# Transposes on TensorE at the start, chunks of last tokens between the parts of Wo, and a later half of the row statistics

## The chip, the core and the metric

The kernel runs on one core of one Trainium2 chip. The metric is the device time of one execution in microseconds (us); shown is the median of three runs. One further execution was recorded by the hardware profiler; all times of single instructions come from it. The names of the engines are those of the profile: PE is TensorE (matmuls), PEld its weight loads, DVE VectorE, ACT ScalarE, POOL GpSimd, SP SyncE (which issues DMAs).

## What is computed

A residual stream x of 2048 rows with 512 columns passes four layers: A, B, A, B, each on the layer-normalised x.

```python
def A(x, mem, Wq, Wk, Wv, Wo):            # H = 32 heads of 128, 8 memory rows, segments of 32 rows
    for s in range(64):
        h = concat([mem, x[32*s : 32*s+32]])              # 40 rows
        q, k, v = h @ Wq, h @ Wk, h @ Wv                  # 512 -> 32 x 128 each
        p = softmax(mask(q @ k.T * scale))                # a memory row sees all 40 rows
        o = (p @ v) @ Wo                                  # 4096 -> 512
        mem, out[s] = o[:8], o[8:]                        # the next segment needs mem
def B(x):                                  # gated MLP that mixes rows
    z = gelu(x @ w_in); z1, z2 = halves(z)
    return (z1 * (w_sp @ layernorm(z2) + b_sp)) @ w_out
x = x + A(ln(x)); x = x + B(ln(x)); x = x + A(ln(x)); x = x + B(ln(x))
```

Layer A is a recurrence over 64 segments: segment s + 1 cannot start its projections before segment s has put out its memory rows. All heads' weights stay in SBUF: Wq, Wk and Wv with 4 MB each, Wo with 4 MB.

## The kernel before

**Layer A** is `a_block` (from L653), called once per A layer; `first` is true for the first. Rows come in 16 tiles of 128 rows (`tb`), four segments to a tile (`j4` = 0 to 3). `_Rows.apply` (L193) normalises a tile with mean and reciprocal deviation and has it turned by a DMA transpose (L201) into `hT`, whose columns are the rows of x; 32 columns ahead of them hold the memory rows. Segment s uses 32 columns of `hT`: 8 of memory and 24 of its rows. The last 8 rows of each segment ("last tokens") don't fit in 32 columns; their projections are made for a whole tile at once: `ln_turn` copies the tile's 32 last tokens out of `hT` into `hB` (L620), and `b_units` (L736) multiplies them with Wq, Wk and Wv in six chunks of 16 matmuls (`psb` at L697), two each. The chunks of the next tile are spread over the segments of the present one as fillers: `fill()` takes the next unit of a generator, `more`, at three places of a segment (L1035, L1041, L1070; in the first segment at L1013 and L1024 instead). Chunks alternate between two accumulators in PSUM, `accA` and `accB`; `accB` also serves `psm`, `psV` and `px` of the segment. What must be read out of a chunk waits in the list `copies` and is run at set places, on ScalarE (L758 or L751). For the first tile it is then turned on VectorE (`turns`, L761) or regrouped; for others by a DMA transpose on SP (L763), and V goes through DRAM (`store_v`, `spread_v`).

**A segment** (L889 to L1079) runs on PE in this order: `psQ`, `psm`, `psK` (queries and keys), `psK`/`psV` (values), `psS` (scores), `psO` (sums and outputs), `psT`, then Wo: `px` (L777, heads 0 to 17, in pairs) and `psO` columns 384 to 511 (L784, heads 18 to 31). VectorE and ScalarE fold the parts of px together (`cross` L1053 and L873, `t1` L875), add the rest (`memT` L880) and turn it into the next segment's memory columns (`hT` L881), on which the next `psQ` waits. `Rt` (L1055, L1058) are the reciprocal sums, with which `tok_out` and `last_out` scale the outputs (L997, L1000).

The order of PE, VectorE and ScalarE is that of the program text; POOL and SP keep theirs by the same text but are not part of the hand-written schedule.

**The start.** SP loads the first two row tiles and the memory rows. POOL issues the weight loads in this order: halves 0 of Wq and Wk, halves 1 of Wq and Wk, both halves of Wv, four parts of Wo (heads 0 to 14) and three parts of `Wo_high` (heads 15 to 22, 23 to 30, 31). The two row tiles are normalised and turned by DMA (L201), the memory rows too (L522). `_consts` makes masks and the identity for transposes (L60 to L65) after that. Then the block runs ahead: chunks 0 and 2 of tile 0, chunks 0 and 2 of tile 1, chunks 1 and 3 of tile 0 (L1084 to L1090; the numbers are j of `b_units`: 0 and 1 Wq, 2 and 3 Wk, 4 and 5 Wv). Segment 0 fills with chunks 4 and 5 of tile 0, segments 1 and 2 with the other four of tile 1 (`units1`, L1118).

**Row statistics.** In the first block, segments with j4 = 1 compute mean and variance of the tile after the next: `x_stats` with k = 0 (first half of the columns, L141, in `spare1`), k = 1 (second half, in `spare2`, L1158) and k = 2 (both put together, L143, in `spare3`, L1167). `spare2` stands ahead of `fold` (L1062), `spare3` behind `build_hA` (L1064) and `store_o`. In segments with j4 = 1 of some tiles `spare2` also adds half of a row tile of y (`y_half`, L229).

```python
            run(turns)
            spare2()
            t1 = wk.tile([P, P], F32, name="t1", bufs=1)
            fold(px, cross, t1, beside)
            if s + 1 < NSEG:
                build_hA(s + 1, pw, t1)
            if s > 0:
                store_o(s, pw, t1)
            spare3()
            tok_out(0)
```

## Time and profile before

| | us |
|---|---|
| median of 3 runs (1649.05, 1649.40, 1654.26) | 1649.4 |
| the profiled execution | 1649.51 |
| its span, first to last instruction | 1647.8 |
| first matmul | 17.62 |
| psQ of segment 0, of segment 1 | 32.11, 53.68 |
| psQ of segment 2, of segment 3, of segment 4 | 65.16, 75.32, 85.24 |

In a line of the timeline stand the start (us from the span's start), the time that the instructions took, engine, line of the kernel, operation, output <- inputs, shape, count, and in brackets the idle time of the engine before it with what ended it. Neighbouring instructions of one kind are merged into a line. In a line of the windows stand the stretch, its length, the busy time and number of instructions of each engine (PE, PEld, DVE, ACT, POOL), the granted TensorE clock as a share, the busy share of the 16 DMA engines and GB/s. In the groups of the page stand busy time, mean time of one instruction in ns, and idle time of the engine just before them. Lines of DMA queues give packets, MB and the share of 16 engines' time in the stretch; q0 are the DMAs that POOL issues, q1 those that SP issues.

### The profile page before, as it was taken

Reading aid. Unit: us, or ns where it says so; the run is one execution under the profiler, and the core shown is the slowest. Engines: PE = TensorE matmul, PEld = TensorE weight load, DVE = VectorE, ACT = ScalarE, POOL = GpSimd, SP = SyncE. Lnnn points to the kernel's source line nnn. Section 1 sums busy time; section 2 is a strip of 40 time slices with the busy share of each in tenths; the row PEclk is TensorE's granted clock in tenths of the full one; section 3 lists DMA queues with packets and bytes.
Section 4 is the critical chain, followed back from the end, with each engine's and each line's share of the span. In section 5 each row is a group of like instructions: output and inputs, shape, how many; then the busy total and the mean of one; then the engine's idle time right before and its main releaser. Section 6 shows DMA issues by size and latency. Waiting matters only on the chain.

```text
span 1647.8 us, 87178 instructions
## 1 busy us (share of the span) xinstructions
PE 1590.4 (97%) x39122; PEld 953.7 (58%) x39122; DVE 1183.4 (72%) x2924; ACT 1072.7 (65%) x2278; POOL 289.2 (18%) x604
## 2 busy tenths in 40 slices
PE   4799999999999999999999999999999999999999
PEld 1455555555665666566655565556556666554565
DVE  3677777778887787884467777777788778877722
ACT  2577777777777777661047777777777777776400
POOL 5111111111211122320011111111122112214000
PEclk9999999999999999999999999999999999999999
DMA  9312221212222234276952121112233123335796
GB/s 353 101 42 42 43 42 44 44 42 74 78 55 45 73 84 87 87 190 139 211 168 46 46 45 46 49 46 44 60 88 85 46 58 94 97 63 153 150 198 162
DMA packets 264734, 149.06 MB, mean 90 GB/s; under 512 B 198680, under 2 KB 240784, under 8 KB 264360
## 3 DMA queue, kind: packets, MB, share of 16 engines
q1 hardware_dynamic: 251128, 99.66, 27.6%
q0 software_dynamic: 13232, 43.82, 8.2%
q8 instruction: 307, 5.03, 1.3%
q14 instruction: 67, 0.55, 0.1%
HBM read 59.68 MB, written 37.19 MB: 59 GB/s over the span
## 4 chain that ended last, share of the span: by engine, by line
PE 55%; DVE 2%; issue 0%; ACT 0%; DVEq 0%
PE pg L388 9%; PE psQ L697 7%; PE psK L697 7%; PE psb L697 5%; PE pz L287 5%; PE px L777 4%; PE psm L697 3%; PE psV L697 3%; PE psO L784 3%; PE py L431 2%; PE pwB L796 2%; PE psO L958 1%; PE psO L975 1%; PE psT L967 1%; PE psS L932 1%; PE pw L1211 0%
## 5 line engine op out<-in xcount | busy, mean ns | idle before, releaser
L697 PEld LDWEIGHTS <-hT 128*32 128x32 bf16 x12288 | 339.8, 97 | 299.9 <-DVE hT L881 27.8
L909 DVE STREAM_TRANSPOSE QQ<-rows 128x512 bf16<-128x512 bf16 x256 | 177.6, 694 | 60.0 <-ACT rows L906 59.0
L909 DVE STREAM_TRANSPOSE KA<-rows 128x512 bf16<-128x512 bf16 x256 | 176.0, 688 | 11.6 <-ACT rows L906 6.1
L997 DVE TENSOR_TENSOR uT<-psO,Rt 128x384 bf16<-128x384 f32 x256 | 141.0, 551 | 36.6 <-ACT Rt L1058 35.6
L906 ACT CAST rows<-psQ 128x512 bf16<-128x512 f32 x256 | 142.8, 595 | 28.3 <-PE psQ L697 25.2
L388 PE MATMUL pg<-z,wspT 128*128 128x344 bf16 x1024 | 154.3, 309 | 0.0
L1058 ACT ACTIVATE Rt<-Rt 128x512 f32<-128x512 f32 x256 | 147.2, 622 | 4.0
L697 PE MATMUL psQ<-Wq_sb,hT 128*32 128x512 bf16 x2048 | 136.0, 383 | 10.7 <-DVE hT L881 6.7
L941 ACT ACTIVATE S<-psS 128x224 bf16<-128x224 f32 x256 | 91.5, 358 | 80.6 <-PE psS L936 80.5
L994 DVE TENSOR_TENSOR uT<-psO,Rm 128x128 bf16<-128x128 f32 x256 | 74.7, 292 | 96.6 <-ACT Rm L993 95.9
L867 POOL COPY KX<-old 128x128 bf16<-128x128 bf16 x128 | 70.2, 548 | 392.3 <-PE psS L936 272.7
L777 PEld LDWEIGHTS <-uT 128*32 128x32 bf16 x4608 | 110.5, 96 | 47.5 <-DVE uT L994 31.7
L697 PE MATMUL psQ<-Wk_sb,hT 128*32 128x512 bf16 x2048 | 135.7, 382 | 0.0
L777 PE MATMUL px<-Wo,uT 128*32 128x256 bf16 x3840 | 134.7, 274 | 0.2 <-DMA Wo<-in_A_Wo_dram 0.2
L697 PE MATMUL psm<-Wq_sb,hT 128*32 128x512 bf16 x2048 | 134.4, 379 | 0.0
L697 PE MATMUL psK<-Wk_sb,hT 128*32 128x512 bf16 x2048 | 134.4, 379 | 0.0
L697 PE MATMUL psK<-Wv_sb,hT 128*32 128x512 bf16 x2048 | 134.3, 379 | 0.0
L697 PE MATMUL psV<-Wv_sb,hT 128*32 128x512 bf16 x2048 | 133.6, 378 | 0.0
L784 PE MATMUL psO<-Wo_high,uT 128*32 128x128 bf16 x7168 | 126.7, 220 | 7.0 <-issue 4.4
L1055 ACT ACTIVATE Rt<-psT 128x1024 f32<-128x1024 f32 x128 | 131.2, 1025 | 3.2
L867 POOL COPY KX<-front 128x128 bf16<-128x128 bf16 x126 | 67.5, 542 | 373.2 <-PE psS L936 238.0
L388 PEld LDWEIGHTS <-wspT 128*128 128x128 bf16 x1024 | 100.2, 98 | 53.2
(190 smaller groups left out, 2867.2 us busy)
## 6 DMA issues: line engine op xcount, KB each, us to landing
o_d<-o_sb SPq DMA_DIRECT2D x126, 64.0 KB
vb_d<-front SPq DMA_DIRECT2D x30, 256.0 KB
VX<-vb_d SPq DMA_DIRECT2D x120, 64.0 KB
ln_x<-xd SPq DMA_DIRECT2D x26, 256.0 KB
y_o<-o_d POOLq DMA_DIRECT2D x22, 256.0 KB, 3.3
xd<-y_o POOLq DMA_DIRECT2D x22, 256.0 KB, 2.9
Wq_sb<-in_A_Wq_dram POOLq DMA_DIRECT2D x8, 512.0 KB, 9.3
Wk_sb<-in_A_Wk_dram POOLq DMA_DIRECT2D x8, 512.0 KB, 11.0
```

The costliest lines, as they stand in the source:

```text
L287: nc.tensor.matmul(pz[:, c0:c1], lhsT=xnT[:, kt, :], rhs=w_in_sb[:, kt, c0:c1], start=(kt == 0), stop=(kt == KT - 1))
L388: nc.tensor.matmul(pg[t][:, k, 0:344], lhsT=wsp[t][:, st, :], rhs=z(st, 344 * k, 344 * k + 344), start=(st == 0), stop=(st == NT - 1))
L697: return [nc.tensor.matmul(ps[32 * cg:32 * cg + 32, :], lhsT=lhs(kt, cg), rhs=rhs(kt, cg), start=(kt == 0), stop=(kt == KT - 1), tile_posi ...
L777: nc.tensor.matmul(px[at:at + 32, 0:256], lhsT=lhs[:, h, :], rhs=wo_rhs(h, slice(k + 2, None, -2) if h % 2 else slice(k, None, 2)), start= ...
L784: nc.tensor.matmul(pw[32 * cg:32 * cg + 32, :], lhsT=lhs[:, h, :], rhs=wo_rhs(h, cg), start=False, stop=(h == H - 1), tile_position=(0, 32 ...
L867: eng.tensor_copy(KX[:, :, r].rearrange("p g (k i) -> p i g k", i=4), bs["KTB"][:, r].rearrange("p (i g) k -> p i g k", i=4)[:, :, :, 8 * ...
L906: return r, mms, nc.scalar.copy(r[:], ps)
L909: nc.vector.transpose(out=QQ[:, j % 2, :, 0:32] if j < 2 else KA[:, j % 2], in_=r[:])
L941: return nc.scalar.activation(out=S[:, r], in_=psS[:, r, 0:224], func=ACT.Exp, scale=scale)
L997: nc.vector.tensor_tensor(out=hview(uT_nxt[:], r, 0, 24), in0=oview(r, 8, 32), in1=rview(r, 0, 24), op=ALU.mult)
L1055: nc.scalar.activation(out=Rt[:], in_=psT[:], func=ACT.Ln)
L1058: nc.scalar.activation(out=rt, in_=rt, func=ACT.Exp, scale=-1.0)
```

## The change

Three things, all in layer A of the first block.

1. The identity for transposes is made directly in bf16 and before the first tiles are normalised. For the first two row tiles and the memory rows, `apply` gets a function `turn`: four TensorE transposes of 128 columns each into a PSUM tile, and one copy on ScalarE into `hT` (or `m0T`). The three DMA transposes are gone. In the text, `turn` of a tile stands between its normalisation and the statistics of the next.
2. `units1` (tile 1's last tokens) gets `alone=True`: all chunks use `accA`, each is one unit, its copy follows it. Two of its chunks still run in the prologue. Of the other four, two run in segment 0 ahead of px and two between heads 22 and 23 of Wo, that is between the first and the second part of `Wo_high`; each is followed by its copy on ScalarE, and for the first two by the DMA transposes on SP. Segments 1 and 2 get no fillers.
3. `x_stats` with k = 1 moves from `spare2` to `spare3`.

```diff
@@ _ln_consts
+    c["ident_bf"] = _identity(nc, cp)
...
+def _identity(nc, cp):
+    ident_bf = cp.tile([P, P], BF16, name="ident_bf")
+    nc.gpsimd.memset(ident_bf[:], 0.0)
+    nc.gpsimd.affine_select(out=ident_bf[:], in_=ident_bf[:], compare_op=ALU.not_equal, fill=1.0,
+                            base=0, pattern=[[-1, P]], channel_multiplier=1)
+    return ident_bf
@@ _Rows.apply
-    def apply(self, tb, MV, RS, first=False, x=None):
+    def apply(self, tb, MV, RS, first=False, x=None, turn=None):
...
-        nc.sync.dma_start_transpose(out=t[:, :, 32:32 + P], in_=xn[:].rearrange("t (kt s) -> t kt s", s=P))
+        if turn is None:
+            nc.sync.dma_start_transpose(out=t[:, :, 32:32 + P], in_=xn[:].rearrange("t (kt s) -> t kt s", s=P))
+        else:
+            turn(t[:, :, 32:32 + P], xn[:], P)
@@ the kernel's start
-        nc.sync.dma_start_transpose(out=rows.m0T[:], in_=m0[:].rearrange("t (kt s) -> t kt s", s=P))
...
-        for tt in range(2):
-            _stats(nc, rp, rows.xs[tt], MV[0][:, tt, :])
-            _rstd_act(nc, RS[0][:, tt:tt + 1], MV[0][:, tt, 1:2], c)
-            rows.apply(tt, MV[0], RS[0], first=True)
+        with tc.tile_pool(name="turn_ps", bufs=3, space=PSUM) as turn_ps:
+
+            def turn(out, x, n):
+                ps = turn_ps.tile([P, KT * n], BF16, name=f"turn{n}", tag="turn")
+                for kt in range(KT):
+                    nc.tensor.transpose(ps[:, n * kt:n * kt + n], x[:, P * kt:P * kt + P], c["ident_bf"][0:n, 0:n])
+                nc.scalar.copy(out, ps[:].rearrange("p (kt t) -> p kt t", kt=KT))
+
+            for tt in range(2):
+                _stats(nc, rp, rows.xs[tt], MV[0][:, tt, :])
+                _rstd_act(nc, RS[0][:, tt:tt + 1], MV[0][:, tt, 1:2], c)
+                rows.apply(tt, MV[0], RS[0], first=True, turn=turn)
+            turn(rows.m0T[:], m0[:], 2 * M)
@@ b_units
-        def b_units(tb, early=0):
+        def b_units(tb, early=0, alone=False):
...
-                ps = (accB if k % 2 and not (now and j == 5) else accA).tile([P, 512], F32, name="psb")[:]
-                for kts in (((0,), (1, 2), (3,)), ((0, 1, 2, 3),))[k % 2]:
+                ps = (accB if k % 2 and not alone and not (now and j == 5) else accA).tile([P, 512], F32, name="psb")[:]
+                for kts in (((0,), (1, 2), (3,)), ((0, 1, 2, 3),))[k % 2 or alone]:
...
-                        elif j == 4:
+                        elif j == (5 if alone else 4):
                             store_v(bs)
...
-                if now or k % 2:
+                if now or k % 2 or alone:
                     yield
@@ wo_rest
-        def wo_rest(pw, lhs):
+        def wo_rest(pw, lhs, lo=WO_PAIR, hi=H):
-            for h in range(WO_PAIR, H):
+            for h in range(lo, hi):
@@ segment
             run(copies)
+            if first and s == 0:
+                ahead_of_wo()
             px = accB.tile([P, 512], F32, name="px")
             wo_pairs(px, uT_cur)
             pw = psO[0][:, 0, 384:512]
-            wo_rest(pw, uT_cur)
+            if first and s == 0:
+                wo_rest(pw, uT_cur, hi=wo.low + 8)
+                ahead_of_wo()
+                wo_rest(pw, uT_cur, lo=wo.low + 8)
+            else:
+                wo_rest(pw, uT_cur)
@@ the prologue of the block
-            units, units1 = b_units(0, 6), b_units(1, 2)
-            for gen in (units, units1, units):
-                for _ in range(4):
+            units, units1 = b_units(0, 6), b_units(1, 2, alone=True)
+            for gen, n in ((units, 4), (units1, 2), (units, 4)):
+                for _ in range(n):
...
+        def ahead_of_wo():
+            for _ in range(2):
+                next(units1)
+                run(copies)
@@ the loop over segments
+            elif first and s == 1:
+                more = iter(())
             elif j4 == (first and tb == 0):
-                more = units1 if first and s == 1 else b_units(tb + 1)
+                more = b_units(tb + 1)
@@ spare2, spare3
-                if first and j4 == 1 and tb + 2 < NB:
-                    x_stats(tb + 2, 1)
...
                 if first and j4 == 1 and tb + 2 < NB:
+                    x_stats(tb + 2, 1)
                     x_stats(tb + 2, 2)
```

More of the change, by code (lines that the diff above doesn't have):

```diff
@@ L59, in _consts @@
     tmp = tctx.enter_context(tc.tile_pool(name="consts_tmp", bufs=1))
-    ident_f = tmp.tile([P, P], F32, name="ident_f")
-    nc.gpsimd.memset(ident_f[:], 0.0)
-    nc.gpsimd.affine_select(out=ident_f[:], in_=ident_f[:], compare_op=ALU.not_equal, fill=1.0,
-                            base=0, pattern=[[-1, P]], channel_multiplier=1)
-    ident_bf = cp.tile([P, P], BF16, name="ident_bf")
-    nc.vector.tensor_copy(ident_bf[:], ident_f[:])
     maskf = tmp.tile([P, 224], F32, name="maskf")
@@ L99, in _consts @@
     tctx.close()
-    c.update(ident_bf=ident_bf, maskN=maskN, ones=ones)
+    c.update(maskN=maskN, ones=ones)
     return c
```

## The prediction

> **What bounds the kernel now.** Read first the page: how full is TensorE, and what does the chain that ended last consist of?
>
> ```profile
> span 1647.8 us, 87178 instructions
> PE 1590.4 (97%) x39122; PEld 953.7 (58%) x39122; DVE 1183.4 (72%) x2924; ACT 1072.7 (65%) x2278; POOL 289.2 (18%) x604
> ```
>
> TensorE works 97% of the span. Moving work can pay only where TensorE idles or runs slowly. Its timeline over the first 100 us shows such a place, segment 0 and the start of segment 1:
>
> ```profile
> 38.87 0.40 PE L697 MATMUL psb<-Wv_sb,hB 128*32 128x512 bf16 x4 [0.83 <-DMA Wv_sb<-in_A_Wv_dram]
> 40.17 0.40 PE L697 MATMUL psb<-Wv_sb,hB 128*32 128x512 bf16 x4 [0.90 <-DMA Wv_sb<-in_A_Wv_dram]
> ...
> 44.12 0.23 PE L958 MATMUL psO<-E,ones 64*128 64x64 bf16 x4 [2.20 <-DVE E L944]
> ...
> 44.76 0.84 PE L777 MATMUL px<-Wo,uT 128*32 128x256 bf16 x24
> 45.78 0.40 PE L777 MATMUL px<-Wo,uT 128*32 128x256 bf16 x6 [0.18 <-DMA Wo<-in_A_Wo_dram]
> 48.78 0.40 PE L777 MATMUL px<-Wo_high,uT 128*32 128x256 bf16 x6 [2.61 <-DMA Wo_high<-in_A_Wo_dram]
> 48.91 0.55 PE L784 MATMUL psO<-Wo_high,uT 128*32 128x128 bf16 x20
> 51.80 1.15 PE L784 MATMUL psO<-Wo_high,uT 128*32 128x128 bf16 x36 [2.34 <-DMA Wo_high<-in_A_Wo_dram]
> 53.68 1.90 PE L697 MATMUL psQ<-Wq_sb,hT 128*32 128x512 bf16 x16 [0.74 <-DVE hT L881]
> ```
>
> Every step to 51.80 is paced by weights that land; the chain is the load stream and then the last heads of Wo. The stages say whether that stream is full (last two columns) and what the clock does (third last):
>
> ```profile
> 5.00:10.00 5.00, 0.00 (x0) 0.00 (x0) 2.81 (x11) 0.50 (x2) 4.49 (x15) 1.00 1.00 308
> 42.70:46.10 3.40, 1.80 (x48) 1.13 (x48) 1.86 (x6) 0.59 (x2) 0.44 (x2) 1.00 1.02 347
> 46.10:49.50 3.40, 0.75 (x28) 0.50 (x26) 0.28 (x1) 0.26 (x1) 0.00 (x0) 1.00 1.03 347
> 49.50:52.90 3.40, 1.10 (x36) 0.88 (x35) 0.29 (x1) 2.17 (x3) 0.00 (x0) 0.50 0.22 72
> 52.90:56.30 3.40, 2.66 (x32) 1.01 (x32) 1.96 (x7) 0.59 (x1) 0.00 (x0) 0.50 0.00 0
> ```
>
> The DMA engines are busy without a break (share 1.00 and more) to 49.5. After a stretch with 0.75 us of matmuls the granted clock falls to 0.50, and stays there into segment 1, whose first 16 matmuls take 1.68 us (53.68 to 55.36) where others take 0.86.
>
> Now the segments that the change touches, cut at the first psQ matmul of each: segments 1, 2, 3, and three with j4 = 1.
>
> ```profile
> 53.68:65.16 11.48, 11.48 (x292) 6.20 (x296) 8.23 (x21) 6.29 (x14) 1.40 (x3) 0.88 0.01 4
> 65.16:75.32 10.16, 10.16 (x296) 5.84 (x292) 7.18 (x19) 8.18 (x20) 1.50 (x3) 1.00 0.25 36
> 75.32:85.24 9.92, 8.64 (x266) 5.24 (x258) 7.55 (x19) 7.76 (x18) 1.51 (x3) 1.00 0.27 76
> 340.53:350.69 10.16, 10.16 (x299) 5.95 (x294) 8.08 (x22) 7.91 (x18) 1.49 (x3) 1.00 0.20 61
> 381.96:392.34 10.38, 10.33 (x297) 5.90 (x293) 8.65 (x24) 8.14 (x18) 3.14 (x6) 1.00 0.36 109
> 587.91:598.29 10.38, 10.33 (x296) 5.80 (x295) 9.08 (x26) 8.39 (x20) 3.13 (x6) 1.00 0.37 120
> ```
>
> The third row matters most: segment 3 has no unit of last tokens in it, 30 matmuls fewer, and is only 0.24 us shorter. A segment without such a unit waits 1.28 us (9.92 - 8.64) where one with a unit computes. **So taking units out of segments 1 and 2 saves almost nothing by itself.**
>
> **Part 1, turning by TensorE.** Three DMA transposes go (two row tiles, memory rows). Two things could follow: last tokens are ready earlier, and the load stream is relieved. First the price of the replacement, from the places where the kernel does the same:
>
> ```profile
> L407 PE MATMUL pT<-ident_bf,front x12: 219/219/229, 839.1 to 1641.9; 128*128 128x128 bf16 x12
> L408 ACT COPY front<-pT x2: 800/808/817, 840.1 to 1642.2; 128x768 bf16<-128x768 bf16 x2
> ...
> 17.27 0.30 ACT L620 COPY hB<-hT 128x128 bf16<-128x128 bf16 x1 [10.79 <-DMA hT<-ln_xn]
> ```
>
> Four transposes and a copy of 512 columns are about 0.6 + 0.6 us a tile, all while TensorE has nothing (its first matmul is at 17.62) and ScalarE has been idle 10.79 us. The second tile's statistics now queue behind the first's copy on ScalarE, which I follow to hB at 11.3 us instead of 17.27 and 24.20. Cost nothing; the cover is 6 us. Nor does earlier hB gain by itself, since the weights of its units land later than that. The gain is the stream:
>
> ```profile
> q0 software_dynamic: 1404, 5.10, 92.9%
> q1 hardware_dynamic: 1261, 0.39, 12.1%
> ...
> q0 software_dynamic: 1573, 5.73, 102.8%
> ```
>
> The first two rows are 10 to 24.2 us, the last 24 to 38. Queue q1 takes 12.1% of 14.2 us, 1.72 us, of which a load of 128 KB is 0.32 at 410 GB/s: 1.4 us for the transposes. The other way: 5.10 MB at the later 5.73/14.0 are 12.46 us instead of 14.2, less 0.32: 1.42. I take 1.4; the bounds are 0 (the stream was held elsewhere) and 1.75.
>
> In segment 0, Wv's last piece then lands at 38.8 instead of 40.17, the prologue (whose last chunks waited for no weights) is ready before that, and the px step is reached at 43.4 instead of 44.76. Against that, two transposes of rowsB are now issued on SP in segment 0, ahead of Wo's end. In segment 1 to 2 (66 to 69.5 us) they and an o_d store took this:
>
> ```profile
> q1 hardware_dynamic: 653, 0.19, 47.6%
> ```
>
> That is 1.67 us of all engines. They start about 46 and 48 us and drain at q1's 12% beside q0, so of the last 3 us of Wo they cost 0.3; bounds 0 and 1.67.
>
> **Part 2, four chunks between the parts of Wo.** A chunk is 16 matmuls, 0.86 us (32.99 to 33.85 in the timeline). All four use one accumulator, so the next waits for the copy: 0.59 us, and I add 0.2 us around it.
>
> ```profile
> 28.68 0.59 ACT L758 CAST rowsB<-psb 128x512 bf16<-128x512 f32 x1 [1.12 <-PE psb L697]
> 49.50 1.02 ACT L1055 ACTIVATE Rt<-psT 128x1024 f32<-128x1024 f32 x1
> 52.99 0.29 DVE L880 TENSOR_TENSOR memT<-psO,t 128x128 bf16<-128x128 f32 x1 [3.10 <-PE psO L784]
> ```
>
> First pair: 43.4 + 0.86 + 0.8 + 0.86 = 45.9; the 30 px matmuls to 46.7; the wait for Wo_high's first part ends at 48.78 - 1.4 = 47.4. Then 26 matmuls to 48.0 and the second pair to 50.5. The last part would land at 51.8 - 1.4 + 0.3 = 50.7. One thing speaks against it:
>
> ```profile
> q8 instruction: 307, 5.03, 1.3%
> ...
> q8 instruction: 1, 0.02, 6.8%
> ```
>
> 307 packets for 78244 TensorE instructions (matmuls and weight loads) are one per 255: these are TensorE's own instructions, and one (33 to 34 us, 6.8% of 16 engines) holds one DMA engine 1.09 us. Before, the third came at 50.4, after the loads. Now 24 instructions of turning (12 transposes, each with a weight load) and 64 of the first pair run ahead of px, so it comes 88 instructions, 44 matmuls, sooner: of the 56 matmuls between 44.76 and 49.4 only 12 stay ahead of it. It falls near 47 us, while the last part is on its way, and that engine's share lands 1.1 us later: 51.7. I take this.
>
> The 36 matmuls then run at full clock, since TensorE now works in the gaps: 0.7 us instead of 1.15. The copy of the fourth chunk and cross on ScalarE end at 51.6, before the matmuls (with the early landing they would end later and set the end, at 52.6 in place of 53.1, and Rt's 1.02 us behind them would then cost segment 1 about 0.5: the same sum). memT and its turn take 0.7: psQ at 53.1. Gain **0.55**; bounds -0.5 and 1.6.
>
> Segment 1 at full clock and without units is a segment 3: 9.92 instead of 11.48, **1.56**; bounds 0 and 1.56. Segment 2 becomes one as well: **0.24**; bounds 0 and 0.25.
>
> **Part 3, the second half of the row statistics.** It stands on VectorE ahead of cross in 14 segments (j4 = 1, first block). Segment 37:
>
> ```profile
> 431.98 0.42 DVE L141 BATCH_NORM_STATS2 bnst<-ln_x 128x6 f32<-128x256 bf16 x1
> 432.16 0.26 ACT L1053 COPY cross<-px 64x128 f32<-64x128 f32 x1 [0.76 <-PE px L777]
> ...
> 432.43 0.28 DVE L873 COPY cross<-px 64x128 f32<-64x128 f32 x1
> ...
> 432.72 0.39 PE L697 MATMUL psb<-Wq_sb,hB 128*32 128x512 bf16 x4
> ...
> 433.16 1.05 PE L697 MATMUL psb<-Wk_sb,hB 128*32 128x512 bf16 x16
> ```
>
> VectorE starts cross 0.27 us after ScalarE started its half, and the Wk chunk (same accumulator as px) starts 0.22 us late. Only the segments that also add a half of y have it: four, 381.96 the first and 587.91 the last, 0.22 over the usual 10.16. Elsewhere statistics end 0.1 us before px does and moving them gains nothing. 4 x 0.21 = **0.84**; bounds 0 and 1. Later, the 0.42 us stand ahead of tok_out, where VectorE then idles about a microsecond for the next segment's rows: nothing.
>
> **Sum.** The profiled execution took 1649.51 (span 1647.8), 0.1 over the median of 1649.4. 0.55 + 1.56 + 0.24 + 0.84 = 3.2, so 1646.3 for it and **1646.2** beside the median.
>
> **Rivals.**
> *The clock falls again.* Around the last landing TensorE works about 1.3 us in 3.4. The rows have full clock kept after 1.80 us in 3.4 and lost after 0.75; between them nothing is shown. If it falls, segment 1 keeps its 1.56: 1647.8. The Trainium skill ("TensorE: Matmul & The Clock Gate", Part 1: The HAM clock gate) has the gate close after an idle window of about 3.4 us; by that rule this rival would be out. But the rows 46.10 to 52.90 lose the clock after a window that was not idle, so it keeps a chance.
>
> *Slower: the chunks run at half clock.* If the prologue, thinner now, leaves TensorE at 0.50 through segment 0, each chunk takes 1.72. Px begins at 43.4 + 4.3 = 47.7, Wo_high's 26 matmuls end at 50.1, the second pair at 54.4, the last heads at 55.5, psQ at 56.2, 2.6 late; segments 1 and 2 give back 0.25 each, part 3 0.84: 1650.7. It decides as soon as half clock lasts past 43 us. Against it: from psQ on (32.11 before, earlier now) segment 0 has five chunks in a row that wait for no weights, 8 us at half clock, and 2.66 us in 3.4 were enough at 52.90 to 56.30.
>
> *More than the sum.* Had the transposes also slowed 5 to 10 us (308 GB/s against 410 later), another 1.25 comes with them. And TensorE waits for its own issue inside Wo's heads:
>
> ```profile
> L784 PE MATMUL psO<-Wo_high,uT 128*32 128x128 bf16 x7168 | 126.7, 220 | 7.0 <-issue 4.4
> ```
>
> Those 4.4 us hang on where instruction packets end in a segment, and 24 instructions shift that everywhere. If a third goes as well: 1646.2 - 1.25 - 1.4 = 1643.6. It can as well rise by as much.
>
> *Part 3 only moves the wait* (tok_out late, then the next rows): 1647.0. Against it stands VectorE's idle time there.
>
> **Chances.** Forecast 0.50; more than the sum 0.22; clock falls 0.13; part 3 moves the wait 0.07; half clock 0.08. The range takes the lower bounds (1.6 + 1.56 + 0.25 + 1 and the issue waits, 5.8: 1643.5, and some scatter) and reaches to the slower rival: 1643 to 1650.6. 0.3% (4.9 us, about what a measurement of this kernel can tell from no change; one of its three runs was 4.9 over the others) lies at 1644.5 and 1654.3. Faster by more: the third rival and the low end of the forecast, 0.28; slower by more: only the half clock with an unlucky run, 0.06; within: 0.66.
>
> **What would show it.** Right: no DMA wait of hB; TensorE's wait for Wv still there but ending about 38.8; chunks at 43 to 50 with two waits for Wo_high much shorter; PEclk 1.00 from 35 to 60; segments 1 and 2 at 9.9; segments 33, 37, 49, 53 at 10.2. Wrong: Wv's last wait still at 40.2 (the stream gained nothing), PEclk 0.50 anywhere in 43 to 60, psQ of segment 1 later than 53.7, or DVE late in segments 34, 38.

## The result, and the profile after

On one chip the changed kernel took 1645.05 us (median of 10 runs, 1641.75 to 1648.32) and the kernel before 1649.68 (10 runs, 1648.57 to 1654.56). The ratio is 0.9967, 95% interval 0.9955 to 0.9978: 5.4 us less by the ratio (3.6 to 7.4), 4.6 by the medians. The forecast was 3.2. The profiled execution took 1644.70, with a span of 1643.0.

| psQ of segment | 0 | 1 | 2 | 3 |
|---|---|---|---|---|
| before | 32.11 | 53.68 | 65.16 | 75.32 |
| after | 30.38 | 53.85 | 63.87 | 73.90 |

Segment 0 ends 0.2 us later than before, where 0.55 earlier was forecast; segments 1 and 2 give 1.45 and 0.13. The timeline of TensorE shows why. Lines of the kernel after stand some 13 higher than before (L697 is now L710, L777 L790, L784 L797, L881 L894); L536 is the new transpose:

```profile
6.53 0.59 PE L536 MATMUL turn<-ident_bf,ln_xn 128*128 128x128 bf16 x4 [6.53 <-POOL ident_bf L59]
...
30.38 1.90 PE L710 MATMUL psQ<-Wq_sb,hT 128*32 128x512 bf16 x16 [1.70 <-DVE hT L211]
...
43.28 0.23 PE L971 MATMUL psO<-E,ones 64*128 64x64 bf16 x4 [2.23 <-DVE E L957]
...
43.92 1.21 PE L710 MATMUL psb<-Wq_sb,hB 128*32 128x512 bf16 x16
45.81 1.90 PE L710 MATMUL psb<-Wk_sb,hB 128*32 128x512 bf16 x16 [0.68 <-ACT rowsB L771]
47.46 1.36 PE L790 MATMUL px<-Wo,uT 128*32 128x256 bf16 x30
48.55 0.38 PE L790 MATMUL px<-Wo_high,uT 128*32 128x256 bf16 x6
...
49.03 1.04 PE L710 MATMUL psb<-Wv_sb,hB 128*32 128x512 bf16 x16
50.76 1.05 PE L710 MATMUL psb<-Wv_sb,hB 128*32 128x512 bf16 x16 [0.69 <-ACT front L764]
51.62 0.69 PE L797 MATMUL psO<-Wo_high,uT 128*32 128x128 bf16 x36
53.85 1.05 PE L710 MATMUL psQ<-Wq_sb,hT 128*32 128x512 bf16 x16 [1.54 <-DVE hT L894]
```

No line from 43 us on waits for a DMA any more: both waits for Wo_high are gone, the last heads (51.62) follow the fourth chunk at once. What paces the end is the chunks themselves. The first pair, 43.92 to 47.46, runs mostly at half clock (1.90 us for 16 matmuls). At the end psQ waits 1.54 us for hT where it waited 0.74 before; the timelines of ScalarE and VectorE have the reason:

```profile
7.83 0.29 ACT L633 COPY hB<-hT 128x128 bf16<-128x128 bf16 x1
...
9.99 0.30 ACT L633 COPY hB<-hT 128x128 bf16<-128x128 bf16 x1
...
51.86 0.58 ACT L764 CAST front<-psb 128x512 bf16<-128x512 f32 x1 [1.15 <-PE psb L710]
52.47 0.26 ACT L1073 COPY cross<-px 64x128 f32<-64x128 f32 x1
52.76 0.29 DVE L888 TENSOR_TENSOR t<-px,cross 128x128 f32<-128x128 f32 x1 [3.49 <-ACT cross L1073]
```

The copy of the fourth chunk stands ahead of cross, and VectorE's half of the fold waits for cross until 52.76. The first two lines are hB of the two tiles: 7.83 and 9.99 us instead of 17.27 and 24.20.

The stretches of TensorE's clock, then segments 1 and 2 (third last column: granted clock):

```profile
31.00:34.43 3.43, 3.43 (x36) 1.26 (x32) 0.71 (x1) 0.98 (x2) 2.12 (x3) 0.50 1.03 411
...
41.26:44.67 3.41, 1.39 (x34) 0.79 (x34) 2.44 (x8) 1.01 (x4) 0.85 (x3) 1.00 1.01 345
44.67:48.08 3.41, 2.73 (x36) 1.22 (x32) 0.03 (x1) 0.92 (x2) 0.00 (x0) 0.50 1.04 346
...
53.85:63.87 10.02, 8.64 (x260) 5.31 (x260) 7.73 (x19) 7.22 (x16) 1.36 (x3) 1.00 0.13 37
63.87:73.90 10.03, 8.64 (x260) 5.27 (x260) 7.99 (x21) 7.42 (x18) 1.30 (x3) 1.00 0.04 10
```

The clock falls after a stretch with 1.39 us of matmuls, is back at 48.08, and segment 1 runs at full clock: 10.03 us instead of 11.48.

The first of these rows is one more loss. The clock is also at half from 27.60 to 34.43, and segment 0 begins in it: its first 48 matmuls (psQ, psm) take 4.58 us (30.38 to 34.96), where they took 2.60 before (32.11 to 34.71). The line of before:

```profile
32.11 1.05 PE L697 MATMUL psQ<-Wq_sb,hT 128*32 128x512 bf16 x16 [1.49 <-DVE hT L206]
```

Over the whole kernel the page's row of Wo's last heads has 2.5 us of waits in place of 7.0:

```profile
L797 PE MATMUL psO<-Wo_high,uT 128*32 128x128 bf16 x7168 | 125.9, 219 | 2.5 <-issue 1.9
```

The wait of 2.34 us at 51.80 is gone from it, and its issue waits fell from 4.4 to 1.9. Whether the change brought the latter was the first question for the experiments.

### The profile page after: what moved, and what is told of

It is laid out like the page before. It is cut to its first block, busy times and chain, and to the rows that moved or that the text cites. A ratio compares the mean times of both kernels' runs of the same rounds, so it can differ in the third digit from the quotient of the medians.

```text
span 1643.0 us, 87201 instructions
## 1 busy us (share of the span) xinstructions
PE 1593.0 (97%) x39134; PEld 945.6 (58%) x39134; DVE 1181.5 (72%) x2923; ACT 1072.8 (65%) x2281; POOL 288.1 (18%) x604
## 4 chain that ended last, share of the span: by engine, by line
PE 55%; DVE 1%; ACT 0%; issue 0%; DMA 0%; SPq 0%; DVEq 0%
PE pg L393 9%; PE psQ L710 7%; PE psK L710 7%; PE psb L710 5%; PE pz L292 5%; PE px L790 4%; PE psm L710 3%; PE psV L710 3%; PE psO L797 3%; PE py L436 2%; PE pwB L809 2%; PE psO L971 1%; PE psO L988 1%; PE psT L980 1%; PE psS L945 1%; PE pw L1237 0%
## 5 line engine op out<-in xcount | busy, mean ns | idle before, releaser
L710 PEld LDWEIGHTS <-hT 128*32 128x32 bf16 x12288 | 332.4, 97 | 309.0 <-DVE hT L894 28.5
L710 PE MATMUL psQ<-Wq_sb,hT 128*32 128x512 bf16 x2048 | 135.1, 382 | 13.1 <-DVE hT L894 9.0
L790 PEld LDWEIGHTS <-uT 128*32 128x32 bf16 x4608 | 110.8, 96 | 44.5 <-DVE uT L1007 32.2
L710 PE MATMUL psQ<-Wk_sb,hT 128*32 128x512 bf16 x2048 | 135.7, 383 | 0.0
L710 PE MATMUL psm<-Wq_sb,hT 128*32 128x512 bf16 x2048 | 135.0, 381 | 0.0
L790 PE MATMUL px<-Wo,uT 128*32 128x256 bf16 x3840 | 134.8, 274 | 0.0
L710 PE MATMUL psK<-Wk_sb,hT 128*32 128x512 bf16 x2048 | 133.9, 379 | 0.0
L710 PE MATMUL psK<-Wv_sb,hT 128*32 128x512 bf16 x2048 | 133.9, 379 | 0.0
L710 PE MATMUL psV<-Wv_sb,hT 128*32 128x512 bf16 x2048 | 133.2, 378 | 0.0
L797 PE MATMUL psO<-Wo_high,uT 128*32 128x128 bf16 x7168 | 125.9, 219 | 2.5 <-issue 1.9
```

The costliest lines, as they stand in the source:

```text
L710: return [nc.tensor.matmul(ps[32 * cg:32 * cg + 32, :], lhsT=lhs(kt, cg), rhs=rhs(kt, cg), start=(kt == 0), stop=(kt == KT - 1), tile_posi ...
L790: nc.tensor.matmul(px[at:at + 32, 0:256], lhsT=lhs[:, h, :], rhs=wo_rhs(h, slice(k + 2, None, -2) if h % 2 else slice(k, None, 2)), start= ...
L797: nc.tensor.matmul(pw[32 * cg:32 * cg + 32, :], lhsT=lhs[:, h, :], rhs=wo_rhs(h, cg), start=False, stop=(h == H - 1), tile_position=(0, 32 ...
```

## The experiments

Each kernel was compared with the kernel before on its own chip. That took 1646.35 us on the chip of before_again, after_again, stats_only and turn_only, 1646.23 on that of chunks_only, turn_stats, early_pair and extra_turns, and 1648.26 on that of copy_late, early_copy_late, spread4 and pad_only. Starts of psQ are those of each profiled execution:

| kernel | psQ 0 | psQ 1 | psQ 2 | psQ 3 | median us | ratio to before, 95% interval |
|---|---|---|---|---|---|---|
| before_again | 33.53 | 55.16 | 66.81 | 76.96 | 1647.38 | 1.0009 (0.9999 to 1.0020) |
| stats_only | 32.04 | 53.34 | 66.28 | 76.44 | 1646.05 | 0.9993 (0.9984 to 1.0002) |
| pad_only | 32.12 | 53.16 | 65.15 | 75.31 | 1648.38 | 1.0000 (0.9991 to 1.0009) |
| chunks_only | 34.70 | 55.07 | 65.09 | 75.12 | 1647.15 | 1.0006 (0.9996 to 1.0017) |
| turn_only | 29.82 | 51.27 | 63.75 | 74.03 | 1643.16 | 0.9978 (0.9969 to 0.9987) |
| turn_stats | 29.61 | 51.23 | 63.74 | 73.90 | 1641.64 | 0.9976 (0.9967 to 0.9985) |
| after_again | 29.83 | 53.28 | 63.31 | 73.34 | 1641.28 | 0.9974 (0.9964 to 0.9985) |
| extra_turns | 32.17 | 55.67 | 65.70 | 75.73 | 1641.89 | 0.9979 (0.9968 to 0.9991) |
| early_pair | 29.74 | 52.88 | 62.90 | 72.93 | 1640.99 | 0.9967 (0.9957 to 0.9977) |
| copy_late | 29.65 | 51.35 | 61.38 | 71.40 | 1644.21 | 0.9970 (0.9959 to 0.9981) |
| early_copy_late | 28.93 | 52.20 | 62.23 | 72.25 | 1642.18 | 0.9961 (0.9947 to 0.9976) |
| spread4 | 30.23 | 52.27 | 63.27 | 73.30 | 1643.28 | 0.9968 (0.9954 to 0.9983) |

Until psQ of segment 3 the first three do the same work as the kernel before (the pad's transposes aside): 75.3 to 77.0, with 75.32 a mean of 76.0. The changed kernel has 73.90 and 73.34, mean 73.6. So the start is worth about 2.4 us in the profiles (the four differ by 1.7 among themselves, the two by 0.6), against a forecast of 0.55 + 1.56 + 0.24 = 2.35.

### The same two kernels again: before_again, after_again

No edit: the kernel before, and the changed one, as they are.

> The kernel before, unchanged, profiled once more. Question: are TensorE's waits for its own issue inside Wo's heads (4.4 us in the first profile, in segments 4, 17, 31, 35, 48, 58, 65, 69, 113, 127) a property of the program or of an execution? Theory A (the program: where its blocks of 256 instructions end): the same segments, 4.4 us within 0.5. Theory B (an execution): other segments, another sum. Time ratio 1.000 within 0.001.

> The changed kernel, unchanged, profiled once more. Its first profile gained 4.8 us of span, of which 1.3 by segment 5, 0.85 by the statistics and 2.5 by issue waits (1.9 instead of 4.4). Theory A (the shift of 24 instructions moves the block ends): issue waits 1.9 within 0.5 in the same segments, and the half clock of segment 0 (27.6 to 34.4 and 44.7 to 48.1 us) may differ. Theory B: issue waits elsewhere, and the sum anywhere between 1.5 and 5. Time ratio to before 0.9967, between 0.9955 and 0.998.

The rows of Wo's last heads, from the pages of before_again and of after_again:

```profile
L784 PE MATMUL psO<-Wo_high,uT 128*32 128x128 bf16 x7168 | 126.1, 220 | 4.9 <-issue 2.6
```

```profile
L797 PE MATMUL psO<-Wo_high,uT 128*32 128x128 bf16 x7168 | 124.7, 219 | 2.5 <-issue 2.0
```

One program has 4.4 us of issue waits in one execution and 2.6 in another. The 4.4 us that the prediction put down to the layout of the program are for a good part the execution's: in both traces the ten waits stand at a few places of a block of 256 TensorE instructions (by the trace's count the 193rd or 194th, in before_again also the 182nd or 183rd), but they hit for the most part other blocks and last 0.15 to 1.17 us. The clock's fall in the first pair came again (44.03 to 47.44), and psQ of segment 1 (53.28) was again later than in the two kernels that have the turn and not the chunks (51.27 and 51.23, below): both are no accident of one profile.

### Does the place of the instructions count: pad_only

```diff
+        ident = rp.tile([P, P], BF16, name="ident_pad")
...
+        with tc.tile_pool(name="turn_ps", bufs=1, space=PSUM) as turn_ps:
+            ps = turn_ps.tile([P, P], BF16, name="pad")
+            for _ in range(12):
+                nc.tensor.transpose(ps[:], ident[:], ident[:])
```

> The kernel before with 12 unused transposes of a 128x128 tile on TensorE at the start, so that all its later TensorE instructions stand 24 places later, as in the changed kernel, and nothing else is moved. It tests the part of the rival 'more than the sum' by which Wo's issue waits (4.4 us in the page of before) hang on that place. My theory: those waits differ from execution to execution of one program (4.7 and 2.9 us in two of the kernel before, 2.5 and 2.5 in two of the changed one), and the time is that of before within 0.1% (1645 to 1648), waits of 1.5 to 5 us. Rival: the place decides, the waits fall to 2.5 and the time by 1.5 to 2.5 us, ratio 0.9985 to 0.9990.

Ratio 1.0000. From its page:

```profile
L792 PE MATMUL psO<-Wo_high,uT 128*32 128x128 bf16 x7168 | 126.0, 220 | 6.4 <-issue 3.5
```

With every later instruction 24 places on, the waits are 3.5 us, between those of the two executions of before. The place alone brings nothing that shows, and the rival's 0.9985 to 0.9990 lies outside the interval: it is out.

### Part 3 alone: stats_only

```diff
@@ spare2
-                if first and j4 == 1 and tb + 2 < NB:
-                    x_stats(tb + 2, 1)
@@ spare3
                 if first and j4 == 1 and tb + 2 < NB:
+                    x_stats(tb + 2, 1)
                     x_stats(tb + 2, 2)
```

> The kernel before with the second half of the row statistics in spare3 and nothing else changed. Theory: segments 33, 37, 49 and 53 go from 10.38 to 10.17, 0.84 us together; no other segment changes by its own doing; ratio 0.9995. Rival (the wait only moves): segments 34, 38, 50, 54 become 0.2 longer; ratio 1.000. Rival (an indirect gain of 2 to 3 us): ratio 0.998.

Segment 37 of this kernel in the timeline, and segments 33 and 37 in the windows:

```profile
431.50 0.26 ACT L1053 COPY cross<-px 64x128 f32<-64x128 f32 x1 [0.76 <-PE px L777]
431.50 0.28 DVE L873 COPY cross<-px 64x128 f32<-64x128 f32 x1
```

```profile
382.22:392.38 10.16, 10.16 (x297) 5.94 (x293) 8.36 (x23) 7.91 (x18) 3.13 (x6) 1.00 0.32 102
422.98:433.14 10.16, 10.16 (x297) 5.81 (x296) 8.79 (x25) 8.18 (x20) 3.13 (x6) 1.00 0.35 113
```

Both halves of cross start together, where VectorE was 0.27 us behind. Segments 33, 37, 49 and 53 take 10.16, 10.16, 10.20 and 10.16 instead of 10.38, 10.38, 10.42 and 10.38: 0.88 us. Of the segments after them 38, 50 and 54 keep 10.16 (34 has 10.29 here, and 10.17 and 10.36 in the two executions of before). So the wait goes and doesn't come back. The time on the whole fits that (0.9993, 1.2 us less) but can't be told from no change by its interval.

### Part 1 alone: turn_only

The changed kernel's identity, `turn` and the loop over the first two tiles put into the kernel before; chunks and statistics as before.

> The kernel before with the two row tiles and the memory rows turned by TensorE and nothing else changed. Theory: the stream of weights is 1.2 to 1.4 us earlier, so Wo_high's two parts end their waits at 47.5 and 50.4 instead of 48.8 and 51.8, psQ of segment 1 at 52.3, and as nothing fills the gaps the clock falls as before and segment 1 keeps 11.4: gain 1.3, ratio 0.9992. Rival (the whole gain is here, through instructions that are shifted by 24 in every later segment): ratio 0.997 to 0.998 and issue waits of about 2 instead of 4.4.

```profile
44.62 1.89 PE L790 MATMUL px<-Wo,uT 128*32 128x256 bf16 x30
...
49.39 1.15 PE L797 MATMUL psO<-Wo_high,uT 128*32 128x128 bf16 x36 [1.87 <-DMA Wo_high<-in_A_Wo_dram]
51.27 1.90 PE L710 MATMUL psQ<-Wq_sb,hT 128*32 128x512 bf16 x16 [0.74 <-DVE hT L894]
```

```profile
38.88:42.29 3.41, 1.67 (x54) 0.73 (x43) 3.38 (x11) 1.65 (x5) 1.40 (x4) 1.00 1.03 346
42.29:45.70 3.41, 2.20 (x42) 1.44 (x45) 1.65 (x6) 0.59 (x2) 0.03 (x1) 0.50 1.04 351
...
51.27:63.75 12.48, 12.47 (x292) 6.41 (x296) 8.23 (x21) 6.29 (x14) 1.40 (x3) 0.81 0.01 4
```

The last part of Wo_high ends its wait at 49.39 instead of 51.80: 2.4 us of relief, not 1.4. That is no accident of two profiles: the first part of Wo_high lands at 47.99 to 50.37 us in the five executions without the turn and at 46.17 to 46.90 in the eight with it (extra_turns, below, aside), 2.3 us by their means. No wait for Wv is left. Segment 0 ends at 51.27, 1.0 us before the 52.3 that I expected of part 1 alone. But the clock is at half from 42.29 to 55.94, and segment 1 takes 12.48. Segment 0 begins at half clock here too; its psQ does so in all nine executions with the turn (1.90 us in its line) and in none of the five without it (1.05). This one part brings most of the change: its ratio is 0.9978, that of the whole change 0.9974 on the same chip.

### What the DMA transposes cost: extra_turns

```diff
             turn(t[:, :, 32:32 + P], xn[:], P)
+            self.unused = self.pool.tile([P, KT, P], BF16, name="unused", bufs=1)
+            nc.sync.dma_start_transpose(out=self.unused[:], in_=xn[:].rearrange("t (kt s) -> t kt s", s=P))
...
             turn(rows.m0T[:], m0[:], 2 * M)
+            nc.sync.dma_start_transpose(out=rows.unused[:, :, 0:2 * M], in_=m0[:].rearrange("t (kt s) -> t kt s", s=P))
```

> The changed kernel with the three DMA transposes put back into an unused tile beside the TensorE ones: nobody waits for their results. It measures what they cost the load stream by themselves. My theory: the stream is held by them, so Wv's last wait and the last part of Wo_high come 2.3 to 2.5 us later than in the changed kernel (40 and 52 instead of 37.7 and 49.8 in the profile's time), the last heads wait for the last part, and psQ of segment 1 is 0.5 to 1.5 us later. As predicted on record: 1.4 us later landings. Rival, that the stream gained by hB's earlier arrival or by chance and not by the transposes: landings within 0.5 us of the changed kernel, and its time.

Nobody waits for these three. The DMA queues from 10 to 24.2 us, after and in this kernel (packets, MB, share of 16 engines):

```profile
q0 software_dynamic: 1578, 5.74, 101.0%
q1 hardware_dynamic: 104, 0.09, 1.8%
```

```profile
q0 software_dynamic: 1406, 5.13, 93.4%
q1 hardware_dynamic: 1033, 0.35, 10.7%
```

The stream's q0 moves 0.61 MB less in 14.2 us, 1.5 us at 5.74 MB in that time. q1's own share rises by 8.9%, 1.26 us. The rest is that q0's packets got slower: 93.4% for 5.13 MB is 2.59 us a MB, 101.0% for 5.74 is 2.50. The third transpose ran from 26.5 us (each waited for the one before, since they share a tile), and 24 to 38 us lost another 0.3 MB (5.25 MB instead of the changed kernel's 5.59, 0.8 us). The second part of Wo_high lands at 52.6 us, in the two executions of the changed kernel at 49.8 and 49.4. TensorE at the end of segment 0:

```profile
52.59 1.05 PE L713 MATMUL psb<-Wv_sb,hB 128*32 128x512 bf16 x16 [0.69 <-ACT front L767]
53.45 0.69 PE L800 MATMUL psO<-Wo_high,uT 128*32 128x128 bf16 x36
55.67 0.61 PE L713 MATMUL psQ<-Wq_sb,hT 128*32 128x512 bf16 x8 [1.54 <-DVE hT L897]
```

psQ of segment 1 comes 1.8 and 2.4 us later than in the two executions of the changed kernel, psQ of segment 0 as well (1.8 and 2.3): the whole prologue moves with the stream. My theory had 0.5 to 1.5 for the end, because it held the chunks to cover more; they cover nothing, as the prologue is what moved. That the last heads would wait was a miss too: they follow the chunk. The transposes do hold the stream, by more than their own packets; the first part of Wo_high lands at 49.68, back among the executions without the turn.

The time doesn't show these 2 us: it is 0.6 over after_again, and the two intervals overlap. It fits badly with them. By the start (psQ of segment 3 at 75.73, 0.3 us before the mean without the turn) and the statistics (0.9), extra_turns should be 1.2 us faster than the kernel before; by its ratio it is 3.5 (1.5 to 5.3). So it is shown that the transposes hold the stream and the start, but not that the gain in the whole time comes from there.

### Part 2 alone, and the change without it: chunks_only, turn_stats

chunks_only is the kernel before with parts 1 and 3 left out of the diff; turn_stats is the changed kernel with `b_units`, `units1`, `wo_rest` and the fillers of segments 1 and 2 as before.

> The kernel before with part 2 alone: hB still comes from DMA transposes, the statistics stay where they were. My theory: the load stream ends as late as before (last part of Wo near 51.7 in the profile's time), the two chunks ahead of px are hidden by it or nearly so, the two between the parts of Wo keep TensorE at full clock behind them; segment 0 ends 0 to 1.5 us later than before, segment 1 takes 10.0 instead of 11.5, segment 2 10.0 instead of 10.2, and the sum to psQ of segment 3 is 0.2 to 1.7 us less than before (ratio 0.999 to 1.000). Rival, that the chunks in Wo are only worth it because of part 1: psQ of segment 1 is over 2 us later than before and segment 3 begins no earlier (ratio 1.000 or over).

> The changed kernel without part 2: the four chunks are fillers in segments 1 and 2 again. With part 1 alone, psQ of segment 3 came at 74.03 (profile's time), with all three parts at 73.33 and 73.90 in two executions. My theory: part 2 is worth 0.1 to 0.7 us, so this kernel is within 0.7 us of the changed one (1642 to 1643 where the changed one has 1641.5). Rival, that part 2 brings what I predicted for segments 1 and 2, 1.8 us, and the rest of the difference is scatter: 1.5 us or more over the changed one.

chunks_only reaches segment 3 at 75.12, 0.2 us before the kernel before and 0.9 before the mean: segment 1 took 10.02, segment 0 ended at 55.07. But segment 0 began late in this profile, at 34.70 instead of 32.11, with the clock at half from 23.30 to 33.54; so this profile doesn't tell how much of the late end the chunks in Wo have caused. No gain in time (1.0006). turn_stats is at 73.90 and 1641.64 us, 0.4 over after_again, its ratio 0.9976 beside 0.9974. So part 2 is worth 0.0 to 0.6 us at segment 3: what it takes from segments 1 and 2 (12.51 + 10.16 there, 10.03 + 10.03 with it, 2.6 us) it adds to the end of segment 0 (51.23 there, 53.28 and 53.85 with it).

### Where the end of segment 0 goes: copy_late

```diff
-                ahead_of_wo()
+                ahead_of_wo(True)
...
-        def ahead_of_wo():
-            for _ in range(2):
+        def ahead_of_wo(last=False):
+            for k in range(2):
                 next(units1)
-                run(copies)
+                if not (last and k):
+                    run(copies)
```

> The changed kernel, with the copy of the fourth chunk left to the next place where copies are run, behind cross and Rt on ScalarE. My theory: in the changed kernel this copy (0.58 us) stands between the last chunk and cross, and with it cross starts 0.5 us after the last heads' matmuls begin to be enough; without it psQ of segment 1 waits 0.8 to 1.0 us for hT instead of 1.54, so it comes 0.5 to 0.6 us earlier, and the whole is 0.5 us shorter at most (within scatter of the changed kernel's 1641.3). Rival, that the last part of Wo_high or the matmuls themselves set the end: hT's wait and psQ unchanged within 0.1.

```profile
43.47 1.05 PE L710 MATMUL psb<-Wq_sb,hB 128*32 128x512 bf16 x16
45.21 1.05 PE L710 MATMUL psb<-Wk_sb,hB 128*32 128x512 bf16 x16 [0.69 <-ACT rowsB L771]
...
49.92 0.69 PE L797 MATMUL psO<-Wo_high,uT 128*32 128x128 bf16 x36
51.35 1.05 PE L710 MATMUL psQ<-Wq_sb,hT 128*32 128x512 bf16 x16 [0.74 <-DVE hT L894]
```

```profile
41.11:44.52 3.41, 1.68 (x34) 0.80 (x34) 2.17 (x7) 0.75 (x3) 0.56 (x2) 1.00 1.02 347
```

hT's wait falls from 1.54 to 0.74: the copy cost 0.8 us. Another 1.2 comes from the clock, which stays full here: the pair takes 2.6 us (43.47 to px at 46.07) instead of 3.5, and from px to the last heads go 3.85 us instead of 4.16. The last 0.45 was gained ahead of the pair, which starts at 43.47 instead of 43.92 (psQ of segment 0 at 29.65 instead of 30.38). The code up to that place is the same as in the changed kernel; 1.68 us of matmuls fell into the stretch, 1.39 there. psQ of segment 3 is at 71.40, 2.5 us ahead of the profile of the changed kernel. Its time on the whole, 0.9970, is the changed kernel's all the same: I can't show this gain beyond the profile.

### Chunks in waits that are there: early_pair, early_copy_late, spread4

```diff
@@ early_pair: segment, ahead of sums_memory(1); the call ahead of px is gone
-            if not (first and s == 0):
+            if first and s == 0:
+                ahead_of_wo()
+            else:
                 fill()
@@ spread4: as early_pair, and
+            if first and s == 0:
+                wo_pairs(px, uT_cur, hi=wo.low)
+                next(units1)
+                run(copies)
+                wo_pairs(px, uT_cur, lo=wo.low)
...
                 wo_rest(pw, uT_cur, hi=wo.low + 8)
-                ahead_of_wo()
+                next(units1)
```

early_copy_late is early_pair with the edit of copy_late.

> The changed kernel with the first pair of chunks moved from ahead of px to ahead of the second half's sums and outputs, where TensorE waits 2.2 us for VectorE's E. My theory: segment 0's end was lost because the pair stands on the path (44 to 47.5 in the profile's time) and the clock fell to half in it after that idle stretch; in the wait the pair costs at most 0.5 us, px begins near 44.5 instead of 47.5, the second pair near 47, the last heads start when the last part of Wo_high lands (near 49.5 to 50.2), and psQ of segment 1 comes near 51.5 to 52.3 instead of 53.85 and 53.28: 1 to 2 us off the whole. Rival, that the clock falls as soon as TensorE waits for the parts of Wo, wherever the pair is: half clock in 45 to 55, segment 1 over 11 us, and no more than 0.5 us off the whole. Second rival, that the copies on ScalarE delay the path from S to E: E over 0.6 us late, and nothing gained.

> The pair in the wait for E, as in early_pair, and the fourth chunk's copy left behind cross and Rt. early_pair had psQ of segment 1 at 52.88 and of segment 3 at 72.93 in the profile's time; its second pair ran partly at half clock. My theory: hT's wait 1.54 becomes 0.8 to 1.0, psQ of segment 1 comes at 52.2 to 52.4, and of segment 3 at 72.3; the whole 0.5 us under early_pair (1640.5). Rival, that the last part of Wo_high (landing 49.4 to 50.6) sets the end: psQ of segment 1 unchanged at 52.8.

> Each chunk in a wait that segment 0 has anyway: two in the wait for E, the third between heads 14 and 15 (in early_pair TensorE waits 1.92 us there for Wo_high's first part), the fourth between heads 22 and 23, its copy left behind cross and Rt. My theory: segment 0's end is then set by the last part of Wo_high alone (landing 49.4 to 50.6), psQ of segment 1 at 51.2 to 52.2, and the clock stays full if a chunk in every stretch of 3.4 us is enough; segments 1 and 2 at 10.0; psQ of segment 3 at 71.5 to 72.3; the whole 1639.5 to 1640.5. Rival by the clock: the wait of about 2.5 us for the last part lets it fall, segment 1 takes 11 to 12.5, and psQ of segment 3 is at 73 or later, no better than early_pair.

early_pair:

```profile
39.99 1.05 PE L710 MATMUL psb<-Wq_sb,hB 128*32 128x512 bf16 x16
...
43.34 1.05 PE L790 MATMUL px<-Wo,uT 128*32 128x256 bf16 x30
46.31 0.40 PE L790 MATMUL px<-Wo_high,uT 128*32 128x256 bf16 x6 [1.92 <-DMA Wo_high<-in_A_Wo_dram]
...
46.85 1.94 PE L710 MATMUL psb<-Wv_sb,hB 128*32 128x512 bf16 x14
...
52.88 1.05 PE L710 MATMUL psQ<-Wq_sb,hT 128*32 128x512 bf16 x16 [1.54 <-DVE hT L894]
```

```profile
43.33:46.74 3.41, 1.49 (x60) 1.19 (x60) 0.29 (x1) 0.57 (x3) 0.00 (x0) 1.00 1.03 346
```

The first pair is free in the wait for E and px begins at 43.34, four us sooner than in the changed kernel (47.46). The time is lost again: px waits 1.92 us for Wo_high, the stretch has 1.49 us of matmuls, and now the second pair runs at half clock. Theory and rival were each half right. early_copy_late removes the 0.8 us of the copy again (psQ of segment 1 at 52.20). In spread4 all chunks lie in waits, and the last part of Wo_high sets the end:

```profile
46.80 0.40 PE L790 MATMUL px<-Wo_high,uT 128*32 128x256 bf16 x6 [0.94 <-DMA Wo_high<-in_A_Wo_dram]
...
50.59 0.94 PE L797 MATMUL psO<-Wo_high,uT 128*32 128x128 bf16 x36 [2.26 <-DMA Wo_high<-in_A_Wo_dram]
52.27 1.90 PE L710 MATMUL psQ<-Wq_sb,hT 128*32 128x512 bf16 x16 [0.73 <-DVE hT L894]
```

```profile
47.47:50.88 3.41, 1.15 (x37) 0.73 (x33) 0.33 (x2) 2.66 (x5) 0.00 (x0) 1.00 1.51 118
```

The stretch of that wait has 1.15 us of matmuls, the clock falls, and segment 1 takes 11.0: the rival by the clock. The three are at 0.9967, 0.9961 and 0.9968, the changed kernel at 0.9974 and 0.9967: none is shown to beat it.

## Why the prediction was right, and where it was not

**The time** came as forecast in its direction and near its size: 3.2 us of gain forecast, 4.6 and 5.1 by the medians on two chips, 5.4 (3.6 to 7.4) and 4.3 (2.5 to 5.9) by the ratios; 3.2 lies just outside the first interval and inside the second. The gain is between the forecast and the rival "more than the sum". The sum for the start, 2.35 us against 2.4, came out by luck: its terms don't. By the forecast part 1 was to bring 1.4 us and part 2 the other 0.95 (1.56 and 0.24, less 0.85 at the end of segment 0). Measured at segment 3, in one or two profiles each, part 1 alone brings 2.0 (74.03 against the mean of 76.0) and part 2 adds 0.0 to 0.6. And of the prediction's own signs of being wrong, two came in the profile: half clock between 43 and 60 us, and psQ of segment 1 behind 53.7.

**The load stream, 1.4 us: mis-sized.** It was taken from the transposes' own packets. Without them the stream's end came 2.4 us sooner (turn_only); put back, the stretch 10 to 24.2 lost 1.5 us of stream for 1.26 us of packets, as q0 took 2.59 us a MB beside them and 2.50 without. The stretch 5 to 10 us, held at 308 GB/s before, moved to 334 only: 0.3 us of the 1.25 that the rival had there.

**Segment 0's end, 53.1: the step that failed.** In the profile it came at 53.85, in spite of a stream earlier than forecast. Three terms were wrong. The step to the chunks and px was put at 43.4 by Wv's landing alone, as if segment 0 ran at full clock. Its first 48 matmuls ran at half clock and cost 2.0 us more, so that the step came at 43.92 although no wait for Wv was left: more than half of the stream's 2.4 us was lost there. The first pair was put down at full clock, 43.4 to 45.9; it ran 43.92 to 47.46 at half clock in two of two executions. And the fourth chunk's copy was to end before the last heads, so as to be hidden. (The last landing, 51.7, is 51.8 by the prediction's own terms.) The case that I had put in brackets, an early landing with the copy and cross setting the end, is the one that came: with the last part of Wo_high landing in time, the copy costs 0.8 us (copy_late). I had held it the same sum, since Rt would be late in segment 1 instead. It isn't: the early landing was lost behind the chunks, and copy_late ends the segment 2 to 2.5 us sooner, 0.8 of it the copy. Against the mean of the four executions without the turn and the chunks (53.84) the changed kernel's two ends (53.57) are still 0.3 earlier: an earlier stream and the three losses nearly cancel.

**The third instruction packet** of TensorE was forecast near 47 us, with 1.1 us for the last part of Wo_high. It came at 47.85 and the last heads waited for nothing. In spread4 one lies in 47 to 48.5 us:

```profile
q8 instruction: 1, 0.02, 4.7%
```

There Wo_high's second part ends its wait 3.79 us behind the first (46.80, 50.59), against 3.02 before (48.78, 51.80): 0.8 us of the 1.1. All 14 traces fit the mechanism. In the three where the packet begins 0.3 to 0.8 us behind the first part's landing (spread4, early_pair, early_copy_late) the second lands 3.80 to 4.07 us behind the first; in the other eleven, where it begins 0.9 us or more behind it, 2.86 to 3.02. The transposes of rowsB are not the reason, since copy_late has them at the same time as spread4 (47 to 49 us) and its parts lie 2.96 apart. In the changed kernel the packet came 0.95 us behind the first landing and cost nothing.

**Segments 1 and 2: right, as stages.** 1.45 and 0.13 of 1.56 and 0.24. They take 10.03, 0.11 over segment 3's 9.92 before. What segment 1 gains hangs on the execution that it is compared with: it takes 11.48, 11.65, 12.94 and 11.99 us in the four without the turn and the chunks, by how long half clock lasts into it.

**Row statistics: right.** 0.88 us in four segments of 0.84 forecast, and the wait isn't found again later. In the changed kernel segment 34 takes 10.42 and 10.95 us (10.17 and 10.36 before), but TensorE waits for nothing of VectorE's in it; the waits that it has are inside Wo's last heads and put down to issue (0.08 and 0.61).

**The rivals.** *The clock falls again* came true earlier than it was placed: after 1.39 us of matmuls in a stretch, inside the range that the rows of before had left open, but in the first pair and not behind the last landing; its price fell on segment 0, and segment 1 kept its gain. By the Trainium skill ("TensorE: Matmul & The Clock Gate", Part 1: The HAM clock gate) it takes an idle window; the trace disagrees, the longest wait in that stretch being 2.23 us. The same section of the Trainium skill has the window running freely, 3413 ns long, so that the phase decides; with that the traces agree (44.67 to 48.08 is 3.41 us, and the same code kept its clock in copy_late). *Chunks at half clock* was right for the first steps of segment 0, to 34.43, and again for one chunk and a half, not for what lies between; its clock came back before segment 1. *More than the sum*: of its two reasons the stretch 5 to 10 us gave 0.3 us, and the place of the instructions is out, since the issue waits vary by themselves and pad_only has no gain.

**What stays open.** Start (2.4 us) and statistics (0.9) make 3.3 of the 4.6 to 5.1 us. The remaining 1.3 to 1.8 us, one per mille, are not explained, and may be scatter: the interval on the second chip, 2.5 to 5.9, holds 3.3. Segments 64 to 127, which no edit touches, take from 642.5 to 646.1 us in the 14 profiles (psQ of segment 64 to psQ of segment 127), and 645.8 and 643.5 in the two of the kernel before. The issue waits in Wo's last heads run from 1.1 us (early_pair) to 4.4 (before) from one profile to the next, and no run told whether their mean has changed.

## What to carry to other kernels

A DMA transpose beside a full load stream isn't hidden because nobody waits for its result: price it by what the stream moves less. Here the stream's end came 2.4 us sooner without three of them (in the whole time of extra_turns the loss didn't show). Work that is put into a gap of the critical path must bring its read-out along; look at which engine reads it out, and put that behind the path's own instruction there. Where a change is worth a few tenths of a per cent, compare the starts of one stage over several executions: two profiles of one program differed here by 1.6 us at segment 3.

## What was not expected of the hardware

The granted clock changes only in steps of 3.41 us, and a fall goes with the matmuls' share of the stretch ahead of it. In the rows shown, full clock was lost after stretches with up to 1.49 us of matmuls (0.75 before, 1.15 spread4, 1.39 after, 1.49 early_pair) and kept after 1.80 (before). Between, both occurred: 1.67 lost it (turn_only), 1.68 kept it (copy_late), and so did 1.57 in chunks_only:

```profile
43.78:47.19 3.41, 1.57 (x34) 0.80 (x34) 2.28 (x8) 0.85 (x3) 0.67 (x3) 1.00 1.02 346
```

Over the whole of all 14 traces, full clock was lost after each of the 26 stretches with up to 1.42 us of matmuls and kept after every one with 1.76 or more; of the twelve between, six lost it. In the first 70 us half clock ended after stretches with 2.68 us or more and went on after those with up to 2.67 (stats_only). So code with a share between 1.4 and 1.8 us runs at full or half clock by where the stretch falls, which is worth 1 to 2.8 us of segments 0 and 1 here and differs between executions.
